# Rearranging the first batch's hand-over, the filters' return and the last tile of a Fourier-mixing and GELU kernel

## The chip, the cores and the metric

The kernel runs on one core of a Trainium2 chip. The metric is device microseconds of one execution. Before the change three runs took 752.50, 753.77 and 754.98 us; their median is 753.77. One more execution was profiled: it took 753.29 us, of which the profile's span covers 751.5.

The core has engines that run side by side, each with its own queue of instructions in order: TensorE (PE, with weight loads shown as PEld), VectorE (DVE), ScalarE (ACT), GpSimd (POOL) and SyncE (SP), which here only issues DMA transfers. POOL issues DMA transfers too: those that change the type on the way (the inputs are fp32, the kernel's tiles bf16 or fp16). All transfers run on the same 16 DMA engines. Matrix products are written to PSUM, which has eight banks; from there DVE or ACT bring them to SBUF ("evacuate" them).

## The reference

Eight batches of 3008 tokens with 256 channels. A real Fourier transform over the tokens is multiplied by a complex filter per frequency and channel, and transformed back. The result goes through two matrix products with an exact GELU between them:

```
X = rfft(x, axis=1);  y = irfft(X * (filt_r + i filt_i), n=3008, axis=1)      # (8, 3008, 256)
h = y.reshape(24064, 256) @ w_in                                              # w_in (256, 2048)
out = (0.5 * h * (1 + erf(h / sqrt(2)))) @ w_out                              # w_out (2048, 256)
```

## The kernel before

**The transform as four stages of matrix products.** 3008 is 47 x 64. A batch goes through a product with a 47-point table (stage 1), a product with the 64-point table and the twiddles (stage 2), the filter, and the two stages back (3 and 4). Between stages 1 and 2, and between 3 and 4, the data are turned round: for batches 1 to 7 by writing them to DRAM (`R1`, `R2`) and reading them back in another order.

- `s1(b, c)`, stage 1, part c of 4: eight matmuls into four PSUM banks, of which one has the tag "h" and three "f"; four evacuations into the tile `a_sb` (L385, pool `pa`, three buffers); four stores to `R1` on SP's queue (L402).
- `r1(b, c)` reads `b_sb` back from `R1` (L408, SP).
- `s2(b, p)`, p from 0 to 11: two matmuls (L416), then on DVE one product of their result with the filters `F` (L419), into a tile `p12` (pool `pp`, six buffers). Product p needs filters 2p and 2p+1 of 24.
- `s3`, `s3_out`: stage 3 and its stores to `R2` (L445); `r2` reads `d_sb` back (L452); `s4` is stage 4 (L461), which ends in `y_sb`, a ring for two batches.

**Batch 0** has functions of its own (`c1`, `c1t`, `c2`, `c3`, `c3t`, `c4`) that turn the data round on PE by transposes, and builds the tables at the same time. `c2(p)` is its product with the filters (L505), on DVE. Its table of stage 3, `T3`, is made in three parts of eight: `table_3` (transposes on PE), `table_3_copy` (to SBUF), and `table_3_turn`, which makes `T3i` out of `T3` by two multiplications by +1 or -1 (L287, on DVE). `warm_up` issues matmuls on a tile of ones, whose result nobody uses.

**The filters.** `load_filters` brings 24 complex filters per channel into rows 0 to 63 of `F` (POOL's DMA queue, L95). For batch 0 `dup_filters` copies them to rows 64 to 127, two filters at a time (L118). Batches 1 to 7 need them in another order of rows: `save_filters` stores rows 0 to 63 to DRAM (`Fd`, L106, SP), and `load_filters_again(k0, k)` reads filters k0 to k0+k-1 back in the new order, in eight transfers (L113, SP). These overwrite `F`, so they wait until batch 0's `c2` is done with the filters in question.

**The two products.** The tokens are cut into 47 tiles of 512. `mm1(t, jc)` makes one sixteenth of h for tile t: two matmuls of 512 columns (L575) into a bank of tag "h" (three banks), and the GELU on ACT (L578). The second product of a tile, `mm2` (L602), takes 64 matmuls of 256 columns. For tiles 1 to 45 it is `mm2_seven` (L662) in its place: a block product by seven multiplications in place of eight (112 matmuls of 128 columns), which needs sums and differences of quarters of the activations, made on DVE (`sums_1`, L632; `sums_2`, L638; `sums_3`, L645) and of the weights (`weight_sums`, L618, once). Its products are added up on DVE out of two PSUM banks of tag "o" (L675 to L685), and stored. The last tile, 46, has `mm2` with a special end: its last quarter is computed in two halves of 128 columns, each stored by itself (L590 to L596, `store`).

**The order.** Nothing is scheduled by a tool. After batch 0's own stages, the main loop (L872) runs over slots, 16 per tile. Slot 16t + jc first calls what the table `at` has for it, then one sixteenth of tile t-1's second product, then `mm1(t, jc)`. `put(slot, f, ...)` fills the table; within a slot the calls run in the order of the `put`s. Those of batch 1 come first (L834): `s1` at slots 0, 4, 8 and 12, `r1` at 15 for parts 0 to 2, `s2` from slot 22 on (product 4 at slot 34), `r2` at 59, `s4` from 67 on, every 0.75 slots. Then come the last tables, the second part of the filters' return and the weight sums at slot 17. The program's order is the order on each engine's queue.

Of the kernel before, what the change touches and what calls it, by code (L numbers as in the profile page):

```python
# [10 lines left out]
ALU = mybir.AluOpType  # L11
FP32 = mybir.dt.float32
# [10 lines left out]
TCH = 512  # L23
# [7 lines left out]
class _Mix:  # L31
# [251 lines left out]
    def table_3_turn(self, q):  # L283

        k = slice(8 * q, 8 * q + 8)
        for r in range(2):
            self.nc.vector.tensor_scalar(out=self.T3i[:, k, r, :], in0=self.T3[:, k, 1 - r, :],  # L287
                                         scalar1=self.turn[r], scalar2=None, op0=ALU.mult)
# [91 lines left out]
    def s1(self, b, c):  # L380

        nc = self.nc
        if c == 0:
            self.st[b, "R1"] = self.dram.tile([NB, 48, 256], BF16, tag="R1", name="R1")
        a = self.pa.tile([128, 2, 4, 256], BF16, tag="a", name="a_sb")  # L385
        x = self.st[b, "x"]
        ps = [[self.bank("ps_s1", "h" if i == h == 0 else "f") for h in range(2)] for i in range(2)]
        for i in range(2):
            for r in range(2):
                for h in range(2):  # L390
                    w = 8 * c + 4 * r + 2 * i
                    nc.tensor.matmul(ps[i][h][64 * r:64 * r + 64, :], lhsT=self.T1s[64 * h:64 * h + NA],  # L392
                                     rhs=x[64 * h:64 * h + NA, w:w + 2, :], start=True, stop=True)
        for i in range(2):
            for h in range(2):
                self._evac(a[:, h, 2 * i:2 * i + 2, :].rearrange("p a b -> p (a b)"), ps[i][h],
                           "act" if h and (b > 1 or i) else False)
        o = self.st[b, "R1"].rearrange("n q c -> q n c")
        for r in range(2):
            for h in range(2):  # L400
                w = HB * h + 8 * c + 4 * r
                nc.sync.dma_start(out=o[:, w:w + 4, :], in_=a[64 * r:64 * r + 48, h])  # L402
# [177 lines left out]
    def mm2(self, t, s):  # L580
# [3 lines left out]
        last = t == self.B * self.S // TCH - 1  # L584
        if last and tile_i == 3:

            half = q // 2
            if q % 2 == 0:
                self.st["o"] = self.bank("ps_e", "o")
            ps = self.st["o"][:, 0:128]  # L590
            for jc in range(8 * (q % 2), 8 * (q % 2) + 8):
                nc.tensor.matmul(ps, lhsT=g[:, jc, 384:512], rhs=self.w_out_sb[:, jc, 128 * half:128 * half + 128],
                                 start=(jc == 0), stop=(jc == 15))
            if q % 2 == 1:
                self.store(t, 3, ps, slice(128 * half, 128 * half + 128))
            return  # L596
# [7 lines left out]
        if last and s == 11:  # L604
            self.store(t, 2, ps[:, 0, :], slice(0, 256))
        elif s % 8 == 7:
            ost = self.po.tile([128, 2, 256], FP32, tag="ost", name="ost")
            nc.vector.tensor_copy(out=ost, in_=ps)
            r0 = t * TCH + (tile_i - 1) * 128
            nc.sync.dma_start(out=self.out[r0:r0 + 256, :].rearrange("(s p) o -> p s o", p=128), in_=ost)  # L610
# [36 lines left out]
    def mm2_seven(self, t, s):  # L647
# [7 lines left out]
               (s31[:, :, 1], q[:, 0]), (a22, q[:, 3]), (s4, w[:, 1, 1]))  # L655
        for n in range(7 * s, 7 * s + 7):
            m, sub, i = n // 16, n // 8 % 2, n % 8
            if n % 16 == 0 and (m == 0 or m % 2 == 1):
                self.st["o"] = self.bank("ps_o", "o").rearrange("p (m s o) -> p m s o", m=2, s=2)
# [4 lines left out]
            if n % 16 != 15 or m % 2:  # L664
                continue
# [10 lines left out]
            elif m == 2:  # L676
                v(out=c(0, 0), in0=t1, in1=p0, op=ALU.add)  # L677
                v(out=t1, in0=t1, in1=p1, op=ALU.add)
            elif m == 4:
                v(out=t3, in0=t1, in1=p0, op=ALU.subtract)  # L680
                v(out=c(1, 1), in0=t3, in1=p1, op=ALU.add)
                v(out=t1, in0=t1, in1=p1, op=ALU.add)
# [7 lines left out]
    def store(self, t, tile_i, ps, cols):  # L690
        ost = self.po.tile([128, 2, 256], FP32, tag="ost", name="ost")
        o = ost[:, 0, 0:cols.stop - cols.start]
        self.nc.vector.tensor_copy(out=o, in_=ps)
        r0 = t * TCH + tile_i * 128
        self.nc.sync.dma_start(out=self.out[r0:r0 + 128, cols], in_=o)
# [3 lines left out]
def kernel(  # L699
# [50 lines left out]
    m.dup_filters(nc.gpsimd, 4, 20)  # L750
    for k in (12, 0):
        m.save_filters(k, 12)
# [3 lines left out]
    for u in range(16):  # L756
# [12 lines left out]
        if u == 11:  # L769
            m.table_2_swap(1)  # L770
            m.table_4(m.T4c, m.T1q, m.wtc, "n", False)
            m.table_3_turn(0)
            m.warm_up(1)
    m.table_3(1)
    m.dup_filters(nc.scalar, 0, 2)
    m.table_3_copy(1, False)
    m.dup_filters(nc.vector, 2, 2)
    m.warm_up(1)
    m.c1t(0, (False, False))
    m.c1t(1, (act,))  # L780
    m.c2(0)
    m.table_3_turn(1)
# [4 lines left out]
    for q in range(1, 7):  # L787
# [7 lines left out]
        if q < 6:  # L795
            m.c3(2 * q - 2)
            if q == 2:
                m.load_filters_again(0, 8)
# [35 lines left out]
    for b in range(1, B):  # L834
        hi = first(b)
        if b == 1:
            s1, n1, r1, s2, n2, group, r2, s4, n4 = 0, 4, 15, 22, 2.5, 12, 59, 67, 0.75
# [24 lines left out]
    put(11, m.table_4_all, g)  # L862
    put(17, m.load_filters_again, 8, 16)
    put(17, m.weight_sums)
    seven = range(1, NT - 1)
# [45 lines left out]
```

## Time and profile before

| what | value |
|---|---|
| median of three runs | 753.77 us |
| profiled execution | 753.29 us |
| its span in the profile | 751.5 us |
| PE busy | 740.1 us, 98% of the span |
| DVE busy | 585.8 us, 78% |
| ACT busy | 545.8 us, 73% |
| POOL busy | 100.8 us, 13%, some two thirds of it in the first 72 us |
| mean granted clock of PE | 0.995 |

The profile names groups of instructions by the line of the kernel, the engine and the tiles: "PE ps_h L575" is the matmul of line 575 that writes the PSUM tile `ps_h`. A releaser, after an arrow, is the instruction or transfer whose end let a waiting one start. "SPq" is the issue of a transfer on SP's queue; "DMA R<-a_sb" is the time until such a transfer has landed. Matmuls overlap: one of 128 columns is listed with 219 ns, but seven in a row take 0.39 us, so the pitch, not the listed duration, is what counts for PE.

In time order: batch 0 and the tables fill the first 38.8 us. There PE, DVE and ACT wait for each other in turn, and `warm_up` keeps PE active. From 38.8 us on the slots run. Batch 1's stages lie among the first 80 slots, up to some 120 us. The DMA engines are nearly full for the first 80 us (x, the filters, both weights, the filters' trip to DRAM and back, batch 1's `R1`). After that each batch runs the same way until the last tile's second product, which begins at 741.7 us and has no first product beside it.

### The profile page before, as it was taken

The numbers are of one execution on the slowest core, as the hardware profiler recorded it, in microseconds if no ns is written. First come the engines' busy times: TensorE is split into PE (matmuls) and PEld (weight loads), VectorE is DVE, ScalarE is ACT, GpSimd is POOL, SyncE is SP. The second block draws the span as 40 slices with busy tenths as digits, with TensorE's granted clock in tenths as the row PEclk, the third lists the DMA queues.
The fourth block names the chain that finished last, engine by engine and source line by source line (L and its number), as shares of the span: only waits on it lengthen the run. The fifth ranks groups of instructions, "written<-read, shape, count | busy, mean of one in ns | idle before, by whom it ended". The sixth has DMA issues, their size and how long they took to land.

```text
span 751.5 us, 20173 instructions
## 1 busy us (share of the span) xinstructions
PE 740.1 (98%) x8388; PEld 518.9 (69%) x8388; DVE 585.8 (78%) x1051; ACT 545.8 (73%) x963; POOL 100.8 (13%) x191
## 2 busy tenths in 40 slices
PE   8989999999999999999999999999999999999998
PEld 4836666766777667667777677666677766777776
DVE  7958977898788977789777997779967798666562
ACT  7866678767786677866777667876678767777773
POOL 7987000021000200012000120002100000000000
PEclk9989999999999999999999999999999999999999
DMA  9999563374434653546526456255562432501011
GB/s 148 225 214 243 149 141 91 115 167 106 113 102 144 151 123 76 142 140 136 123 82 174 106 111 165 58 152 120 122 146 72 135 104 74 127 29 58 30 57 57
DMA packets 91804, 90.71 MB, mean 121 GB/s; under 512 B 7744, under 2 KB 78528, under 8 KB 91456
## 3 DMA queue, kind: packets, MB, share of 16 engines
q1 hardware_dynamic: 83328, 73.43, 35.6%
q0 software_dynamic: 8384, 16.00, 14.0%
q8 instruction: 65, 1.06, 0.6%
q14 instruction: 27, 0.22, 0.1%
HBM read 57.15 MB, written 48.23 MB: 140 GB/s over the span
## 4 chain that ended last, share of the span: by engine, by line
PE 84%; DMA 8%; DVE 4%; POOL 1%; issue 1%; ACT 1%; SPq 1%; DVEq 0%; POOLq 0%; ACTq 0%
PE ps_h L575 38%; PE ps_o L662 34%; PE ps_s L433 3%; PE ps_s L461 3%; PE ps_s L416 2%; DMA R<-a_sb 2%; PE ps_o L602 2%; PE ps_s L392 2%; DVE p L419 2%; DMA F<-Fd 1%; DVE s_sb L632 1%; DMA Fd<-F 1%; DMA w_in_sb<-in_moe_w_in_dram 1%; DMA d_sb<-R 1%; DMA x_sb<-in_x_dram 1%; DMA R<-v_sb 1%
## 5 line engine op out<-in xcount | busy, mean ns | idle before, releaser
L578 ACT ACTIVATE g_sb<-ps_h 128x512 f16<-128x512 f32 x752 | 448.4, 598 | 184.4 <-PE ps_h L575 181.7
L575 PE MATMUL ps_h<-y_sb,w_in_sb 128*128 128x512 bf16 (+3 forms) x1600 | 447.9, 367 | 2.9 <-DVE a_sb L302 2.9
L662 PEld LDWEIGHTS <-g_sb 128*128 128x128 f16 x2880 | 190.2, 98 | 78.7 <-issue 15.6
L662 PEld LDWEIGHTS <-s_sb 128*128 128x128 f16 x2160 | 147.5, 98 | 51.3 <-issue 2.9
L575 PEld LDWEIGHTS <-w_in_sb 128*128 128x128 bf16 x1600 | 124.9, 98 | 10.2 <-issue 5.2
L662 PE MATMUL ps_o<-w_sums,g_sb 128*128 128x128 f16 x1440 | 124.7, 219 | 0.0
L662 PE MATMUL ps_o<-w_sums,s_sb 128*128 128x128 f16 x1440 | 124.5, 219 | 0.0
L632 DVE TENSOR_TENSOR s_sb<-g_sb 128x1024 f16<-128x1024 f16 x180 | 119.4, 686 | 0.0
L662 PE MATMUL ps_o<-w_out_sb,g_sb 128*128 128x128 f16 x1440 | 118.4, 219 | 0.3
L419 DVE TENSOR_TENSOR p<-ps_s,F 128x1024 bf16<-128x1024 f32 x84 | 102.4, 1220 | 17.9 <-PE ps_s L416 16.9
L123 POOL COPY gate<-p 1x1 bf16<-1x1 bf16 x40 | 19.1, 478 | 425.0 <-DVE p L419 425.0
L638 DVE TENSOR_TENSOR g_sb<-s_sb,g_sb 128x1024 f16<-128x1024 f16 x90 | 61.7, 685 | 1.1
L662 PE MATMUL ps_o<-w_out_sb,s_sb 128*128 128x128 f16 x720 | 62.2, 219 | 0.0
L645 DVE TENSOR_TENSOR s_sb<-g_sb 128x1024 f16<-128x1024 f16 x90 | 61.3, 681 | 0.0
L302 DVE CAST a_sb<-ps_s 128x512 bf16<-128x512 f32 x60 | 38.5, 685 | 18.6 <-PE ps_s L392 13.9
L304 DVE TENSOR_SCALAR y_sb<-ps_s 128x376 bf16<-128x376 f32 x56 | 30.5, 545 | 28.8 <-PE ps_s L461 28.8
L461 PEld LDWEIGHTS <-d_sb 96*128 96x128 bf16 x448 | 31.5, 98 | 26.9 <-issue 1.9
L680 DVE TENSOR_TENSOR t_sb<-t_sb,ps_o 128x256 f32<-128x256 f32 x45 | 18.7, 417 | 40.0 <-PE ps_o L662 40.0
L677 DVE TENSOR_TENSOR ost<-t_sb,ps_o 128x256 f32<-128x256 f32 x45 | 18.8, 418 | 31.3 <-PE ps_o L662 31.3
L685 DVE TENSOR_TENSOR ost<-t_sb,ps_o 128x256 f32<-128x256 f32 x90 | 33.6, 414 | 7.4 <-PE ps_o L662 7.4
L461 PE MATMUL ps_s<-T4a,d_sb 96*128 96x94 bf16 x448 | 37.4, 206 | 0.9 <-DMA d_sb<-R 0.9
L86 POOL DMA_DIRECT2D x_sb<-in_x_dram x64 | 33.0, 520 | 2.5 <-issue 2.5
(149 smaller groups left out, 515.1 us busy)
## 6 DMA issues: line engine op xcount, KB each, us to landing
out_dram<-ost SPq DMA_DIRECT2D x93, 256.0 KB, 2.8
x_sb<-in_x_dram POOLq DMA_DIRECT2D x64, 188.0 KB, 3.7
R<-a_sb SPq DMA_DIRECT2D x112, 96.0 KB, 2.2
b_sb<-R SPq DMA_DIRECT2D x28, 384.0 KB, 4.2
R<-v_sb SPq DMA_DIRECT2D x84, 128.0 KB, 2.4
d_sb<-R SPq DMA_DIRECT2D x56, 192.0 KB, 3.9
F<-Fd SPq DMA_DIRECT2D x8, 256.0 KB, 8.3
Fd<-F SPq DMA_DIRECT2D x8, 192.0 KB, 7.7
```

Source lines behind the costliest of these rows:

```text
L86: nc.gpsimd.dma_start(out=xt[h * o:h * o + NA, w:w + 8, :], in_=xv[h][:, w:w + 8, :])
L302: self.nc.vector.tensor_copy(out=out, in_=in_)
L304: self.nc.vector.tensor_scalar(out=out, in0=in_, scalar1=scale, scalar2=None, op0=ALU.mult)
L419: nc.vector.tensor_tensor(out=w, in0=ps.unsqueeze(1).to_broadcast([128, 2, 512]), in1=self.F[:, :, 2 * p:2 * p + 2, :].rearrange("p t a b ...
L461: nc.tensor.matmul(ps[:, 94 * i:94 * i + 94], lhsT=d[:, (grp % 2) * 4 + i, 128 * half:128 * half + 128], rhs=self.T4a[:, 4 * grp + i], sta ...
L575: nc.tensor.matmul(ps[:, o:o + n], lhsT=self.w_in_sb[:, dc, jc * 128:jc * 128 + 128], rhs=self.ring[:, dc, off:off + n], start=(dc == 0), ...
L578: nc.scalar.activation(out=self.st["g", t][:, jc, :], in_=ps, func=AF.Gelu)
L632: self.nc.vector.tensor_tensor(out=self.st["s", t][:, i:i + 2], in0=a, in1=b, op=ALU.subtract)
L638: self.nc.vector.tensor_tensor(out=a21[:, k], in0=self.st["s", t][:, k, 0], in1=a22[:, k], op=ALU.add)
L645: self.nc.vector.tensor_tensor(out=self.st["s4", t][:, k], in0=a12[:, k], in1=s2[:, k], op=ALU.subtract)
L662: nc.tensor.matmul(ps[:, (m + 1) % 2, sub, :], lhsT=a[:, i, 128 * sub:128 * sub + 128], rhs=b[:, i], start=i == 0, stop=i == 7)
L685: v(out=c(h, 1 - h), in0=tt, in1=p, op=ALU.add)
```

## The change

1. `s1(1, 3)`, batch 1's last part of stage 1, writes its evacuations into two tiles of the pool `pp` (the product tiles `p12`) instead of an `a_sb` tile.
2. The return of filters 0 to 7, which stood among batch 0's stages, moves into the slots, in two pieces of four filters: slot 13 and slot 15, the latter behind `r1`. Each piece is eight transfers, so that the return takes 24 transfers instead of 16. On SP's queue the order is now: batch 1's 16 stores of stage 1, eight returns, three `b_sb`, eight returns, and the eight returns of filters 8 to 23.
3. `table_3_turn(1)` runs on POOL, right behind batch 0's `table_3_copy(1)`. The copies of filters 4 to 23 (also POOL) come behind it in the queue; those of filters 0 to 3, of which ACT had one and DVE one, are both on DVE. `c1t(0)` is evacuated half by DVE and half by ACT instead of by DVE alone. One `warm_up` stands a little earlier.
4. Batch 1's `s4` starts at slot 68 instead of 67, with 0.68 instead of 0.75 slots between its 16 calls.
5. The last tile takes `mm2_seven` like the others. There products 5 and 6 are computed in halves of eight matmuls, each half in an output bank of its own, added up and stored by itself (`finish`); the finished quarters of the output are stored early (`store`).

```
     def s1(self, b, c):
...
-        a = self.pa.tile([128, 2, 4, 256], BF16, tag="a", name="a_sb")
+        if b == 1 and c == 3:
+            a = [self.pp.tile([128, 2, 512], BF16, tag="p12", name="p12").rearrange("p i (j c) -> p (i j) c", j=2)
+                 for h in range(2)]
+        else:
+            a = self.pa.tile([128, 2, 4, 256], BF16, tag="a", name="a_sb")
+            a = [a[:, 0], a[:, 1]]
...
     nc.gpsimd.memset(m.vt[:, :, 96, :], 0.0)
-    m.dup_filters(nc.gpsimd, 4, 20)
-    for k in (12, 0):
-        m.save_filters(k, 12)
...
-            m.table_3_turn(0)
+            m.table_3_turn(0, nc.vector)
             m.warm_up(1)
     m.table_3(1)
-    m.dup_filters(nc.scalar, 0, 2)
+    m.dup_filters(nc.vector, 0, 4)
+    m.warm_up(1)
+    m.c1t(0, (False, act))
     m.table_3_copy(1, False)
-    m.dup_filters(nc.vector, 2, 2)
-    m.warm_up(1)
-    m.c1t(0, (False, False))
+    m.table_3_turn(1, nc.gpsimd)
+    m.dup_filters(nc.gpsimd, 4, 20)
+    for k in (12, 0):
+        m.save_filters(k, 12)
     m.c1t(1, (act,))
     m.c2(0)
-    m.table_3_turn(1)
...
-            if q == 2:
-                m.load_filters_again(0, 8)
...
-            s1, n1, r1, s2, n2, group, r2, s4, n4 = 0, 4, 15, 22, 2.5, 12, 59, 67, 0.75
+            s1, n1, r1, s2, n2, group, r2, s4, n4 = 0, 4, 15, 22, 2.5, 12, 59, 68, 0.68
...
+    put(13, m.load_filters_again, 0, 4)
+    put(15, m.load_filters_again, 4, 4)
     put(17, m.load_filters_again, 8, 16)
     put(17, m.weight_sums)
-    seven = range(1, NT - 1)
+    seven = range(1, NT)
...
     def mm2_seven(self, t, s):
...
+        last = t == self.B * self.S // TCH - 1
         for n in range(7 * s, 7 * s + 7):
             m, sub, i = n // 16, n // 8 % 2, n % 8
-            if n % 16 == 0 and (m == 0 or m % 2 == 1):
+            if n % 16 == 0 and (m == 0 or m % 2 == 1) or last and m > 4 and i == 0:
                 self.st["o"] = self.bank("ps_o", "o").rearrange("p (m s o) -> p m s o", m=2, s=2)
...
-            if n % 16 != 15 or m % 2:
+            if last and m > 4 and i == 7:
+                self.finish(t, m, sub, ps)
+            if n % 16 != 15 or m % 2 or last and m > 4:
                 continue
...
+    def finish(self, t, m, sub, ps):
+        h = 6 - m
+        c, tt = self.st["c"][h], self.st["t"][:, h]
+        k = slice(128 * (1 - h), 128 * (1 - h) + 128)
+        self.nc.vector.tensor_tensor(out=c[:, sub, k], in0=tt[:, sub], in1=ps[:, (m + 1) % 2, sub], op=ALU.add)
+        r0 = t * TCH + 256 * h + 128 * sub
+        self.nc.sync.dma_start(out=self.out[r0:r0 + 128, k], in_=c[:, sub, k])
```

## The prediction

> **What bounds the kernel now.** I read the page first: TensorE (PE) is busy for 740.1 of 751.5 us, so at most 11 us can be saved by closing gaps. The slices of the page, then stretches of a few microseconds, show where the gaps lie. In the table by stretches the columns are busy time (and count) of PE, of PE's weight loads, VectorE (DVE), ScalarE (ACT) and GpSimd (POOL), the granted clock, the DMA share and GB/s:
>
> ```profile
> 46.00:48.00 2.00, 2.00 (x14) 0.65 (x13) 0.00 (x0) 1.33 (x4) 1.92 (x3) 1.00 1.32 214
> 48.00:50.00 2.00, 0.27 (x2) 0.00 (x0) 0.00 (x0) 0.00 (x0) 1.84 (x3) 1.00 1.31 215
> 50.00:52.00 2.00, 0.85 (x3) 0.30 (x3) 1.60 (x3) 1.57 (x3) 1.92 (x3) 0.52 1.30 230
> ...
> 56.00:58.00 2.00, 2.00 (x12) 1.26 (x11) 2.00 (x2) 0.96 (x2) 1.92 (x3) 0.77 0.14 27
> 58.00:60.00 2.00, 2.00 (x15) 1.17 (x12) 1.49 (x2) 1.43 (x3) 1.92 (x2) 1.00 0.92 307
> ```
>
> PE stands still from 48.27 to 51.15 (2.88 us), and then runs at half clock until about 56.9: 5.75 us at half speed are another 2.9 us. Together 5.8 us. DMA is full until about 55, and all but idle only from 56 to 58. The chain of waits says why PE stood (start us, us, what):
>
> ```profile
> 32.96 9.74 DMA F<-Fd
> 42.70 0.02 issue
> 42.72 7.56 DMA R<-a_sb
> 50.28 0.03 issue
> 50.31 0.05 DVEq L302
> 50.36 0.04 issue
> 50.40 0.70 DVE a_sb L302
> 51.10 0.04 issue
> 51.15 1.01 PE ps_h L575 x2
> ```
>
> The fourth part of batch 1's first stage (slot 12) needs the `a_sb` buffer of the first part. That buffer's stores stand on SP's queue behind the return of filters 0 to 7 (F<-Fd), and SP's waits list them as released by landings of F<-Fd: a transfer there waits for the one eight places ahead. So the gap is a queueing one. The later steps on SP's queue, from its timeline:
>
> ```profile
> 56.77 1.29 SPq L408 DMA_DIRECT2D b_sb<-R  x3
> 58.11 5.20 SPq L113 DMA_DIRECT2D F<-Fd  x8
> ```
>
> The first b_sb landed 3.3 us after its issue, at 60.1, and PE's first product of batch 1 (slot 22, L416) started at 60.26, without a wait. The last eight F<-Fd landed 6.0 to 10.0 us after issue, the last at 71.9; the first product that needs them runs on DVE at 73.30.
>
> **Edit 1: the fourth part into two product tiles, and filters 0 to 7 returned behind it.** The 7.56 us wait on R<-a_sb leaves the path: two of six product tiles, long free, take its place. In the timeline before, PE ran that part's matmuls at 46.34, so three DVE casts of 0.61 us each end at about 48.85 instead of 52.3. PE then reaches slot 16 at 49.0 (gelus of 0.6 us set the pace) and slot 22 six slots of 0.87 us later (four matmuls of 0.109 and two of 0.216), at 54.2.
>
> What is late next is b_sb. SP now holds, in this order: four stores, eight F<-Fd of filters 0 to 3, three b_sb, eight F<-Fd of filters 4 to 7, eight of filters 8 to 23: 24 returns instead of 16, and eight of them ahead of b_sb. From 48.9: four stores at 0.43 (the pitch of 52.31 to 53.66 before) end at 50.6; eight issues at 0.45 would end at 54.2, and the last four must first see the last stores land (3.0 to 3.5 us after issue), which is about as late. So b_sb is issued near 54.3 and lands 3.3 us later, at 57.6. PE, there at 54.2, waits 3.4 us: the old wait has moved eight slots on. If DMA has less to carry at that time the landing could be 1.5 us earlier; if the small returns (64 KB, for which no row exists) cost as much as the 128 KB ones (1.0 us apart while shared) instead of by bytes (0.3 us, from 8.9 us for eight of 256 KB), it is up to 2.5 us later.
>
> Does that wait cost the clock again? In the stretch from 46.68 to 50.10 PE was busy for 1.59 of 3.42 us, and the clock halved at its end; from 5.72 to 9.14 it was busy for 2.10 and kept the clock. A wait of 3.4 us leaves less than 1.6 us of work in some such stretch unless its phase is lucky. So I count the clock as lost for 5.1 us (between 3.4 and 6.8): 2.6 us. At slot 34: 57.6, plus 12.45 us (60.26 to 72.71 before), plus 2.6, is 72.65 against 72.71. Edit 1 alone gives about 0. With the clock kept it gives 2.6, and with a short wait up to 4.5.
>
> The Trainium skill (TensorE: Matmul & The Clock Gate, Part 1) speaks of at least one idle window of about 3.4 us before the clock drops. The row of this trace differs: 2.88 us of idleness, and a stretch that was 46% busy, were enough. By the page a wait of under 3.4 us would cost no clock and the sum would be 2.6 us lower.
>
> **Edit 2: turns on GpSimd, copies behind them.** The turns (L287, two DVE operations, 0.25 us apart) leave DVE, and the copies of filters 4 to 23 now follow them on POOL. Two rows matter, DVE's and POOL's:
>
> ```profile
> 17.86 3.59 DVE L505 TENSOR_TENSOR p<-ps_c,F 128x1024 bf16<-128x1024 f32 x3
> 18.03 3.98 POOL L118 COPY F<-F 64x1024 bf16<-64x1024 bf16 x4 [1.04 <-DMA F<-in_filt_i_dram]
> ```
>
> DVE's third product of batch 0 starts at 19.09, just as the first copy ends (19.06). The 0.5 us freed on DVE, and the half of `c1t` moved to ACT in exchange for its copy, therefore buy nothing: the copy could not start before its filters landed at 17.9. What can be lost is there: ACT's copy of the table ends near 16.85, POOL's clearing of vt at 16.98, then two turns of 128x512. Their price on POOL is not in the trace. Rows on both sides:
>
> ```profile
> L319 POOL COPY T2p<-T 128x768 bf16<-128x768 bf16 x4 | 3.1, 825 | 0.0
> L376 POOL TENSOR_TENSOR t_sb<-t_sb 96x376 f32<-96x376 f32 x16 | 14.0, 894 | 2.0 <-ACT t_sb L300 1.4
> L333 POOL TENSOR_SCALAR pick<-cols,p 128x128 bf16<-128x128 f32 x1 | 0.6, 632 | 0.1
> ```
>
> By the copy's rate a turn of 512 elements is 0.56 us, by the two-input row (0.19 fixed, as for one element, and 0.70 for 375 more) 1.15, by the 128x128 comparison (0.44 for 127 more) 1.95. I take 0.8, between the first two, which are nearest in size: one bf16 input like the copy, with arithmetic on top. The turns then end at 18.6, the first copy at 19.6, and the chain of DVE products, which runs without a gap to 30.5, is 0.55 us late (0.1 to 2.85). All of batch 0 behind it shifts by that: PE's first gelu matmul from 38.84 to 39.4, and slot 12 with it. The x loads behind the copies on POOL shift too, by less, since the copies also wait for filters at 22.5; DMA has room there (share 0.75 to 0.89 from 28 to 32).
>
> The Trainium skill (GPSIMD Engine Reference, 4.1 Engine selection) keeps elementwise work on VectorE, which speaks against this edit; one-input operations it calls roughly line-rate. The best loop that its section 3.1 states, 1.8 cycles an element, would make an estimate of 0.77 us a turn, and a sum within 0.1 us of mine; no run here shows one yet.
>
> **Edit 3: batch 1's last stage a slot later** (67 to 68, spacing 0.68). The chain shows PE waiting for its input there:
>
> ```profile
> 100.42 4.01 DMA d_sb<-R
> 104.43 0.14 issue
> 104.56 0.51 PE ps_s L461 x8
> ```
>
> PE's gap is 0.77 us; one slot more of work (0.82) covers it. Gain 0.77 (0 if a later d_sb, which lands up to 107.65, is met instead).
>
> **Edit 4: seven products in the last tile.** PE's work falls from 7.04 us (48 matmuls in 5.24, 32 in 1.80) to 112 x 0.056 = 6.25. But at 741.70 DVE still has 0.35 us of the tile before, then five sums (0.60 each, rows L632, L638, L645) and six evacuations (0.375): 5.6 us, near 6.0 with its waits on PE. There are two output banks: product 5's second half needs the one that the third evacuation of product 4 frees, so PE, there after 5.2 us, waits until 6.05; 24 matmuls (1.34), and the last evacuation (0.29, row L693) end at 7.75. Before it was 7.35. So the end is 0.4 us later (0.8 earlier if DVE were never in the way, 0.9 later with sums of 0.69). The last store is 64 KB both times and lands 1.5 us on.
>
> **Sum.** 0.55 (edit 2) - 0.05 (edit 1) - 0.77 + 0.4 = +0.1 on the profiled 753.29 (span 751.5 and 1.8 around it): 753.4. The three runs have 753.77 as median, 0.5 above; half of that kept, 753.6. The likeliest is thus no change that can be told.
>
> **Rivals.** (A) The forecast: a second wait takes the place of the first. By itself 751.8 to 755.8. (B) The second wait is short or keeps the clock: b_sb 1 to 1.5 us earlier, or a lucky phase. For it: DMA was idle from 56 to 58, so its total leaves 2 us; against: eight returns stand ahead of b_sb. It gives -2.6 to -3.5: near 750.6. (C) The return becomes the bound: 16 transfers, not eight, follow b_sb, and product 4 on DVE (73.30 before) needs the last of 24. By bytes the last lands at 71.9 - 2.5 + 8 x 0.3 = 71.8, in time; at 1.0 us each, with those ahead of b_sb late too, near 77.4. DVE has no gap from 66.6 to 80.8, so what exceeds 73.3 goes through to PE: +4, or 757.6. It decides from about 0.7 us a small return. (D) The turns at 1.95 us each: +2.3, near 755.8; it only adds to the others.
>
> **Chances.** A 0.43, B 0.36, C 0.21, with D spread over them. About 0.3%, 2.3 us, is what a measurement of this kernel can tell from no change: below 751.5 is faster, above 756.0 slower. B lies all but wholly below and A all but wholly between: faster 0.37, same 0.42, slower 0.21. The range takes in most of B and a part of C: 749.6 to 756.6.
>
> **What would show it.** No gap at slot 14 near 48; L118 on POOL starting near 18.6; a PE gap ahead of the first L416-type product (57 to 59), released by b_sb, with a second stretch at clock 0.5; no gap ahead of the last stage's first matmul near 104; at the end a PE wait of about 0.8 us between product 5's halves. I am wrong if PE passes slot 22 without a wait, or if F<-Fd lands past 74.

## The result and the profile after

The changed kernel takes 756.75 us (median of four runs, 756.10 to 756.99), the kernel before in the same job 753.39 (752.50 to 754.98). The ratio is 1.0041, with a 95% interval of 1.0022 to 1.006: slower by 3.1 to 3.4 us, where the prediction had 753.6 and "no change" as the likeliest. The profiled execution took 756.71 us, its span 754.9; before it was 753.29 and 751.5, so the two traces show the same difference, 3.4 us. Of all executions behind the ratios below one, of run i1, took 3317.52 us and is left out.

Read in order of time, the trace after says where that is. First the turns, in the groups of GpSimd (POOL) from 15 to 24 us by shape, and behind them the timelines of POOL and DVE (start, us, engine, line):

```profile
L287 POOL TENSOR_SCALAR T<-T,turn_r 128x512 bf16<-128x512 bf16 x1 | 1.6, 1586 | 0.5 <-ACT T L300 0.5
L287 POOL TENSOR_SCALAR T<-T,turn_i 128x512 bf16<-128x512 bf16 x1 | 1.6, 1558 | 0.0
```

```profile
20.43 3.99 POOL L118 COPY F<-F 64x1024 bf16<-64x1024 bf16 x4
```

```profile
21.50 3.49 DVE L510 TENSOR_TENSOR p<-ps_c,F 128x1024 bf16<-128x1024 f32 x3 [3.09 <-POOL F L118]
```

A turn is 1.57 us on POOL, not 0.8. The first copy starts at 20.43 instead of 18.03, DVE's third product at 21.50 instead of 19.09, 2.41 us late, and so does everything behind it: PE's first gelu matmul comes at 41.25 instead of 38.84, late by 2.41 again.

Then the hand-over. The table by stretches of the trace after (columns as before), with SP's timeline of the same time and PE's waits from 36 to 125 us:

```profile
46.00:48.00 2.00, 1.98 (x14) 0.68 (x13) 1.65 (x3) 1.96 (x6) 1.44 (x2) 1.00 1.27 248
48.00:50.00 2.00, 2.00 (x14) 0.67 (x14) 1.02 (x3) 1.97 (x6) 1.84 (x3) 1.00 0.95 267
...
56.00:58.00 2.00, 0.76 (x6) 0.24 (x3) 0.38 (x1) 1.12 (x2) 1.92 (x3) 1.00 0.50 145
58.00:60.00 2.00, 0.00 (x0) 0.00 (x0) 0.00 (x0) 0.00 (x0) 1.92 (x3) 0.74 0.96 277
60.00:62.00 2.00, 1.60 (x7) 1.02 (x8) 0.98 (x1) 0.00 (x0) 1.84 (x3) 0.50 1.02 394
62.00:64.00 2.00, 1.78 (x7) 1.03 (x7) 0.66 (x2) 0.60 (x1) 1.92 (x3) 0.50 0.87 214
64.00:66.00 2.00, 2.00 (x9) 1.13 (x8) 1.41 (x2) 0.60 (x1) 1.92 (x3) 0.56 1.00 250
```

```profile
53.16 3.70 SPq L113 DMA_DIRECT2D F<-Fd  x8
56.96 1.32 SPq L413 DMA_DIRECT2D b_sb<-R  x3
58.37 8.08 SPq L113 DMA_DIRECT2D F<-Fd  x16
```

```profile
PE ps_s L421 <- DMA b_sb<-R: 3.6, 1, 3.6
```

The stop at 48 us is gone, as predicted. A stop of 3.64 us (56.76 to 60.40) for `b_sb` has taken its place, and the clock is lost behind it, from 58.95 to 65.78. That is the likeliest case of the prediction, and yet it is worse than before in one respect. Before, the stop and the lost clock lay *ahead* of `b_sb`, which landed at 60.12; PE arrived at 60.26. There the half clock was all but free. In the experiments below the kernel before was executed 129 times: 37 executions had a mean granted clock of 1.000 and took 752.89 us on average, 17 had 0.995 (some 7 us at half clock) and took 753.37, only 0.5 more. Now `b_sb` lands at 60.26 and the slow clock lies *behind* it: product 4's matmuls start at 75.32 instead of 72.55. The last return lands at 74.31 instead of 71.91.

Stage 4's gap of 0.77 us is gone. When batch 2's first stage begins, the kernel is 2.14 us late, 0.27 less than at the first gelu; at the last gelu 2.18. So from the first gelu to batch 2 the new hand-over costs 0.50 (the 0.77 saved at stage 4, less the 0.27). The rest is at the end. The chain of waits after, last part:

```profile
746.22 2.64 PE ps_o L653 x44
748.86 0.02 issue
748.88 0.43 DVE t_sb L675
749.32 0.02 issue
749.34 0.42 DVE ost L676
749.76 0.34 DVE t_sb L679
750.10 0.05 issue
750.15 1.62 PE ps_o L653 x24
```

From the last gelu to the last evacuation it is 8.17 us instead of 7.32 (+0.85), because the 24 matmuls of the end wait for DVE's third evacuation of product 4 to free a bank. The end of the span comes 1.28 us behind the last landing instead of 0.91 (+0.37, found in every kernel that has the new end, and in none that hasn't; no trace shows why). With the landing itself the time behind the last evacuation is 0.40 longer. Sum: 2.41 - 0.27 + 0.04 + 0.85 + 0.40 = 3.4.

### The profile page after: what moved, and what is told of

The parts are those of the page before. It is cut to its first block, busy times and chain, and to the rows that moved or that the text cites. A ratio compares the mean times of both kernels' runs of the same rounds, so it can differ in the third digit from the quotient of the medians.

```text
span 754.9 us, 20124 instructions
## 1 busy us (share of the span) xinstructions
PE 730.8 (97%) x8284; PEld 518.7 (69%) x8420; DVE 592.9 (79%) x1063; ACT 545.5 (72%) x963; POOL 104.4 (14%) x193
## 4 chain that ended last, share of the span: by engine, by line
PE 87%; DVE 5%; DMA 2%; issue 2%; ACT 2%; POOL 1%; SPq 1%; DVEq 0%; POOLq 0%
PE ps_o L653 37%; PE ps_h L580 36%; PE ps_s L466 3%; PE ps_s L438 3%; PE ps_s L421 3%; PE ps_s L397 2%; DVE p L424 2%; ACT g_sb L583 1%; DVE s_sb L622 1%; PE ps_o L594 1%; DMA x_sb<-in_x_dram 1%; PE ps_c L528 1%; DVE ost L682 1%; DMA d_sb<-R 1%; DMA R<-v_sb 1%
## 5 line engine op out<-in xcount | busy, mean ns | idle before, releaser
L580 PE MATMUL ps_h<-y_sb,w_in_sb 128*128 128x512 bf16 (+3 forms) x1468 | 418.6, 366 | 0.3
L653 PEld LDWEIGHTS <-g_sb 128*128 128x128 f16 x2944 | 193.9, 98 | 81.0 <-issue 15.6
L653 PEld LDWEIGHTS <-s_sb 128*128 128x128 f16 x2208 | 150.3, 98 | 51.4 <-issue 2.9
L653 PE MATMUL ps_o<-w_sums,g_sb 128*128 128x128 f16 x1472 | 127.3, 219 | 2.1 <-DVE t_sb L679 0.9
L653 PE MATMUL ps_o<-w_sums,s_sb 128*128 128x128 f16 x1472 | 126.5, 219 | 1.2
L653 PE MATMUL ps_o<-w_out_sb,g_sb 128*128 128x128 f16 x1472 | 120.4, 219 | 1.8
L622 DVE TENSOR_TENSOR s_sb<-g_sb 128x1024 f16<-128x1024 f16 x184 | 122.0, 687 | 0.0
L628 DVE TENSOR_TENSOR g_sb<-s_sb,g_sb 128x1024 f16<-128x1024 f16 x92 | 63.3, 688 | 1.1
L635 DVE TENSOR_TENSOR s_sb<-g_sb 128x1024 f16<-128x1024 f16 x92 | 62.8, 683 | 0.0
L302 DVE CAST a_sb<-ps_s 128x512 bf16<-128x512 f32 x57 | 36.6, 686 | 14.0 <-PE ps_s L397 13.9
L421 PE MATMUL ps_s<-b_sb,T2p 128*128 128x256 bf16 x168 | 32.5, 276 | 4.7 <-DMA b_sb<-R 3.6
```

The lines of the kernel that those rows point to most:

```text
L302: self.nc.vector.tensor_copy(out=out, in_=in_)
L421: nc.tensor.matmul(ps[:, 256 * i:256 * i + 256], lhsT=self.T2p[:, k].rearrange("p a b c d -> p (a b c d)"), rhs=self.st[b, "b", k // 6][:, ...
L580: nc.tensor.matmul(ps[:, o:o + n], lhsT=self.w_in_sb[:, dc, jc * 128:jc * 128 + 128], rhs=self.ring[:, dc, off:off + n], start=(dc == 0), ...
L622: self.nc.vector.tensor_tensor(out=self.st["s", t][:, i:i + 2], in0=a, in1=b, op=ALU.subtract)
L628: self.nc.vector.tensor_tensor(out=a21[:, k], in0=self.st["s", t][:, k, 0], in1=a22[:, k], op=ALU.add)
L635: self.nc.vector.tensor_tensor(out=self.st["s4", t][:, k], in0=a12[:, k], in1=s2[:, k], op=ALU.subtract)
```

## The experiments

Eighteen kernels were run, each in five rounds beside the kernel before on the same chip. "Ratio" is to that kernel (interval in brackets); 0.1% is 0.75 us. The kernel before took between 752.82 and 753.44 us in these jobs, so times in us of different jobs are compared through the ratios. A profile is one execution, and not always a typical one: that of e1 was the slowest of twelve (757.52), that of h2 the slowest of eleven (754.58), that of b4 the fastest of twelve (752.71).

| run | kernel | median us | before | ratio |
|---|---|---|---|---|
| e1 | change, turns and copies as before | 755.26 | 753.44 | 1.0026 [1.0017, 1.0036] |
| e2 | change, last tile as before | 756.79 | 753.44 | 1.0045 [1.0031, 1.0058] |
| e3 | change, batch 1's products 4 slots later | 756.48 | 753.44 | 1.0039 [1.0026, 1.0053] |
| e4 | change, one of two turns on DVE | 755.65 | 753.44 | 1.0036 [1.0024, 1.0048] |
| b1 | before + hand-over and return (edit 1) | 754.29 | 752.82 | 1.0020 [1.0011, 1.0029] |
| b2 | before + stage 4 later (edit 3) | 751.98 | 752.82 | 0.9993 [0.9984, 1.0002] |
| b3 | before + new last tile (edit 4) | 753.85 | 752.82 | 1.0015 [1.0006, 1.0023] |
| b4 | before + turns on POOL (edit 2) | 753.73 | 752.82 | 1.0015 [1.0006, 1.0025] |
| g1 | e3, batch 2's x loads put later | 755.80 | 753.11 | 1.0033 [1.0021, 1.0045] |
| g2 | b1 + b2, batch 2's x loads put later | 753.68 | 753.11 | 1.0008 [0.9997, 1.002] |
| g3 | before + product tiles alone | 752.74 | 753.11 | 0.9997 [0.9988, 1.0005] |
| g4 | b1, return of 0 to 7 in one piece | 755.05 | 753.11 | 1.0027 [1.0016, 1.0039] |
| h1 | b1 + 13 idle matmuls at slot 21 | 754.64 | 752.83 | 1.0023 [1.0014, 1.0032] |
| h2 | b1, x loads held back | 752.62 | 752.83 | 0.9996 [0.9987, 1.0005] |
| h3 | b1 + b2 + h1 + h2 | 753.32 | 752.83 | 1.0010 [1.0000, 1.0021] |
| h4 | product tiles + b2 | 752.63 | 752.83 | 0.9995 [0.9985, 1.0004] |
| i1 | change, x loads held back | 756.65 | 753.14 | 1.0051 [1.0038, 1.0064] |
| i2 | product tiles + b2, x loads held back | 752.22 | 753.14 | 0.9990 [0.9980, 1.0000] |

### Undoing parts of the change (e1 to e4)

On the changed kernel. In e1 the copies also go back to their old places and engines, in e2 `mm2`, `mm2_seven` and `store` are those of before, in e4 the turn takes the one part `r` that it is to do.

```
e1
-    m.table_3_turn(1, nc.gpsimd)
...
     m.c2(0)
+    m.table_3_turn(1, nc.vector)
e2
-    seven = range(1, NT)
+    seven = range(1, NT - 1)
e3
-            s1, n1, r1, s2, n2, group, r2, s4, n4 = 0, 4, 15, 22, 2.5, 12, 59, 68, 0.68
+            s1, n1, r1, s2, n2, group, r2, s4, n4 = 0, 4, 15, 26, 2.5, 11, 60, 68, 0.68
e4
-    m.table_3_turn(1, nc.gpsimd)
+    m.table_3_turn(1, nc.gpsimd, (0,))
...
     m.c2(0)
+    m.table_3_turn(1, nc.vector, (1,))
```

> The changed kernel with the whole of edit 2 undone: both turns on VectorE after the first product, copies of filters 4 to 23 first on GpSimd, first copies and the first transposes' evacuation as before. Theory 1 (the turns cost 1.58 us each on GpSimd and delay the chain of products from 19.1 to 21.5): third product at 19.1 again, first gelu matmul near 38.8, first b_sb 2 to 2.4 us earlier, time lower by 2.0 to 2.6 us than the changed kernel's 756.7, that is 754.1 to 754.7. Theory 2 (the filters' return is the bound, the last return lands where it does because of 24 transfers): the last return lands within 1 us of 74.3 and the time falls by less than 1 us.

> The changed kernel with edit 4 undone: the last tile has the four-quarter form of before. Theory 1 (in the last tile VectorE's queue and two output banks cost more than the 0.8 us that PE saves): the time from the last gelu to the last evacuation goes from 8.17 back to 7.3 us, and the time falls by 0.8 to 1.3 us, to 755.4 to 755.9. Theory 2 (the tail is a wash): less than 0.4 us.

> The changed kernel with batch 1's filter products four slots later (first at slot 26 instead of 22, groups 11 instead of 12 slots apart, d_sb reads at slot 60 instead of 59). Theory 1 (PE's wait of 3.6 us at slot 22 for b_sb, with the half clock after it, is a wait for a latency chain on SP's queue, and work can be put into it): no PE gap near 57 to 60, no second stretch at half clock, and a time lower by 3.4 to 6.4 us, 750.3 to 753.3; the lower end only if product 4 does not meet the last return (74.3). Theory 2 (transfers bound everything to 75 us): product 4 on VectorE not before 74.3, and less than 1.5 us gained.

> The changed kernel with one of the two turns back on VectorE (after the first product), one on GpSimd ahead of the copies. Theory 1: the third product starts 1.58 us earlier than in the changed kernel, at 19.9, and the time falls by about 1.6 us (1.2 to 2.0). Theory 2: the position of the turns on GpSimd's queue does not set the end; under 0.7 us.

Measured: without the turns on POOL the change is 1.1 us (by the ratios) to 1.5 us (by the medians) better, with one of them moved back 0.4 to 1.1. That is less than the 2.4 us that the turns delay, and the intervals overlap that of the whole change, so no single gain here is clear of noise. The traces show what takes over. DVE's product 4 is the first that needs the last returned filters. In the changed kernel it starts at 75.75, with no idle time before it; in e1:

```profile
74.51 1.22 DVE L424 TENSOR_TENSOR p<-ps_s,F 128x1024 bf16<-128x1024 f32 x1 [1.40 <-PE ps_s L421]
```

PE, the releaser that is named, had been done since 72.27; the last return landed at 74.23 (74.31 in the changed kernel, so this sign is theory 2's). In e1, e2, e3, g1, g2, h1 and h3 DVE stands idle ahead of product 4 and starts it 0.27 or 0.28 us behind the last landing of the return; with the return in its old place no kernel waits there. In the whole change the return is not yet the limit, but it is only 1.2 us away (74.31 plus 0.27, against 75.75): time won ahead of product 4 is kept up to there, unless the return comes earlier too.

e2 gave nothing by the medians, although its trace has the old end of 7.32 us again; the intervals are wide enough to hold the 1.2 us. Its profiled execution began later (first gelu matmul at 42.41) and had its last return at 76.03, which is taken up below. e3 removed the wait for `b_sb`, kept the clock in its profiled execution (its four others were granted 0.997), and gained 0.3: theory 2's number. Product 4 waited 1.68 us for the last return, and the chain of e3 says what held it next:

```profile
75.32 11.28 DMA R<-v_sb
...
102.45 3.82 DMA d_sb<-R
```

The first stores to `R2` (L450) took up to 11 us to land. Transfers, not PE, had become the limit there.

### Each edit alone (b1 to b4)

On the kernel before, one part of the change's diff at a time.

```
b1   (with the new s1)
-                m.load_filters_again(0, 8)
...
+    put(13, m.load_filters_again, 0, 4)
+    put(15, m.load_filters_again, 4, 4)
b2
-            s1, n1, r1, s2, n2, group, r2, s4, n4 = 0, 4, 15, 22, 2.5, 12, 59, 67, 0.75
+            s1, n1, r1, s2, n2, group, r2, s4, n4 = 0, 4, 15, 22, 2.5, 12, 59, 68, 0.68
b3   (with the new mm2, mm2_seven, store, finish)
-    seven = range(1, NT - 1)
+    seven = range(1, NT)
b4   (with the copies behind it, as in the change)
-    m.table_3_turn(1)
+    m.table_3_turn(1, nc.gpsimd)
```

> The kernel before with only the hand-over changed (fourth part of stage 1 into two product tiles, filters 0 to 7 returned in two pieces of eight transfers at slots 13 and 15). Theory 1 (the losses read one by one from the trace of the changed kernel add up; the wait only moves from slot 14 to slot 22 and the clock is lost once either way): 753.4 to 754.1, a gap ahead of the first matmul of batch 1's stage 2 of 2 to 4 us released by b_sb. Theory 2 (eight more return transfers and the later last return are the main cost; DVE's product 4 waits for the last F<-Fd, and the stores to R2 and the read of batch 2's x behind it are late too): 755 to 756, last F<-Fd after 73, DVE's product 4 after 74.

> The kernel before with only batch 1's stage 4 moved (slot 68, spacing 0.68). Theory 1: the gap of 0.77 us ahead of the first L461 matmul goes, 752.5 to 753.0. Theory 2 (a later d_sb, landing up to 107.65, is met instead, or the time is taken elsewhere): 753.2 to 754.

> The kernel before with only the last tile's second product by seven products. Theory 1: from the last gelu to the last evacuation 8.2 us in place of 7.3, and the end of the span 0.4 us further behind it: 754.2 to 754.7. Theory 2 (run e2, which took this edit back without any gain in time, shows what it costs): 753.2 to 753.7.

> The kernel before with only the second pair of turns on GpSimd and the copies of filters 4 to 23 behind it. Theory 1 (two turns of 1.57 us delay the copies by 2.4 us, the chain of DVE products and all behind it shift by as much): first gelu matmul at 41.2 and 755.4 to 755.9. Theory 2 (the delay in batch 0 is hidden later, because PE stands at slot 14 until stores behind the filters' return have landed, and transfers until 72 us set when product 4 runs): first gelu matmul at 41.2 too, the gap ahead of slot 14 shorter than 2.9 us, and 753.4 to 754.4.

Alone they cost +1.5, -0.5, +1.1 and +1.1 us by the ratios, each give or take 0.7, +3.2 together, against 3.1 for the whole. The hand-over, predicted at nothing, is the largest by the ratios, though the intervals overlap. The kernel before was 0.57 us faster in this job than in the first; allowing for that, b2 and b3 are theory 1's, b4 is theory 2's, and b1 lies between its two, near theory 2 by its time, but with its last return at 72.61, not after 73. b3's trace has the same +0.85 and +0.37 as the whole change. b4's first gelu matmul is at 41.23, as late as after, and at batch 2's first stage nothing is left of the delay (119.85 against 119.83). PE's waits in b4 from 36 to 125 us:

```profile
PE ps_s L416 <- DMA b_sb<-R: 1.8, 1, 1.8
PE ps_h L575 <- DVE a_sb L302: 1.2, 1, 1.2
```

The old stop at slot 14 is 1.2 us instead of 2.9, and the clock was kept. So in this execution the delay was hidden in a stop that ended at its own time; where the 1.1 us of the other executions lie, no trace shows. Why the delay can't hide in the whole change is seen by putting all 20 profiled kernels into two groups (us):

| return of filters 0 to 7 | first gelu matmul | first `b_sb` issued | last F<-Fd landed |
|---|---|---|---|
| among batch 0's stages (7 kernels) | 38.2 to 41.2 | 55.8 to 57.6 | 70.8 to 72.7 |
| of these b4, turns on POOL | 41.23 | 56.56 | 71.48 |
| moved into the slots (13 kernels) | 38.8 to 43.3 | 15.5 to 16.5 behind it | 72.1 to 77.0 |
| of these b1 | 39.14 | 54.86 | 72.61 |
| of these after | 41.25 | 56.96 | 74.31 |

With the old order `b_sb` comes when the transfers are through, whenever batch 1 starts. With the new order the return and `b_sb` follow batch 1's stores, and every delay of the start goes through to both (the last return lands 32.9 to 35.1 us behind the first gelu matmul in all 13). Edit 1 brings `b_sb` 1.9 us forward (b1), and edit 2 takes 2.1 back.

### Which half of the hand-over costs (g1 to g4)

g1 is e3, g2 is b1 with b2, each with the x loads put later (g2 from slot 44 on); g3 is the change's `s1` alone; g4 is b1 with its return in one piece.

```
g1
-                put(unit(i + 2) if b > 1 else 25, m.load_next, b, i + 2, i // 2, i % 2)
+                put(unit(i + 2) if b > 1 else 48 + int(2.5 * i), m.load_next, b, i + 2, i // 2, i % 2)
g4
-    put(13, m.load_filters_again, 0, 4)
-    put(15, m.load_filters_again, 4, 4)
+    put(13, m.load_filters_again, 0, 8)
```

> Run e3 (the changed kernel with batch 1's products four slots later, 756.48) with batch 2's eight loads of x moved from slot 25 to slots 48 to 65. Theory 1 (two limits lie close together: b_sb with the lost clock, and the transfers, which are full until 82 to 86 us because the x loads of batch 2 run beside the filters' return and the first stores to R2; e3 took the first away and met the second, 11.28 us of DMA R<-v_sb in its chain): those stores take 2 to 4 us, the gaps after 80 us go, 752.9 to 755.0. Theory 2 (the middle of the kernel is not bound by transfers, e3 gained nothing for another reason): 756 to 757.

> The kernel before with the hand-over of the change and its later stage 4, and batch 2's x loads at slots 44 to 61; turns and last tile as before. Theory 1: b1 (754.29) without its 1.48 us wait of DVE's v_sb for R<-v_sb and without the gap ahead of stage 4, 751.5 to 753.0, so it beats the kernel before by 0 to 1.5 us. Theory 2: as b1 and b2 together, 753.5 to 754.2.

> The kernel before with the fourth part of stage 1 in two product tiles and nothing else; the return of filters 0 to 7 stays among batch 0's stages, as eight transfers. Theory 1 (the loss of the hand-over lies in the return, whose eight more transfers stand ahead of b_sb and go out at SP's pitch of 0.46 us each, with the last landing at 72.6 in b1 although b_sb was issued 1.9 us earlier): b_sb is issued at 53.5 to 55, the gap ahead of stage 2 is under 3 us, the last F<-Fd lands before 71, and the time is 751.0 to 752.8. Theory 2 (the loss lies in the tiles, or in the clock that any wait near 55 costs): 753.5 to 754.5, as b1.

> Run b1 with filters 0 to 7 returned in one piece at slot 13 (eight transfers of 128 KB instead of sixteen of 64 KB). Theory 1 (the number of transfers counts): the last F<-Fd lands 2 to 4 us earlier than in b1 (72.6), b_sb up to 1 us later, 752.8 to 754.0. Theory 2 (bytes count): landings as in b1, 754.0 to 754.8.

g1 and g2 did not test what they were made for. GpSimd issues a load as soon as its queue is empty, and in g2 the x loads went out at 68.5 to 72.2 us, as in the kernel before (67.5 to 71.1), whatever their slot. g3 answers: the product tiles alone cost nothing, so the 1.5 us lie in moving the return. They also win nothing that can be told (two of theory 1's signs failed: `b_sb` was issued at 56.96 and the last return landed at 72.27), and its waits of PE show the next thing behind the old one:

```profile
PE ps_o L607 <- DMA w_out_sb<-in_moe_w_out_dram: 3.2, 2, 2.8
PE ps_s L421 <- DMA b_sb<-R: 1.9, 1, 1.9
```

With the return in its old place the weights of the second product land at 55.04 (48.32 in b1), and PE stands 2.8 us for them where it stood 2.9 for `a_sb`. g4 refutes theory 1 there: eight transfers in place of sixteen were no better. The last return came 0.5 us earlier, `b_sb` 1.7 us later, and PE stood for 5.3 us.

### Clock or transfers (h1 to h4)

`keep_busy` issues matmuls of 128x512 from `w_in_sb` into a PSUM bank that nobody reads. In h2 `load_next` puts a small POOL copy of a product tile ahead of a load, as it does for the later batches, so that POOL's queue waits for that product.

```
h1
+    put(21, m.keep_busy, 13)
h2
     def load_next(self, b, p, c, h):
-        if b > 1:
+        if b > 0:
             self.gate(self.st[b, "p", p][0:1, 0, 0:1])
...
-                put(unit(i + 2) if b > 1 else 25, m.load_next, b, i + 2, i // 2, i % 2)
+                put(unit(i + 2) if b > 1 else unit(i + 4), m.load_next, b, i + 2 if b > 1 else i + 4, i // 2, i % 2)
```

> Run b1 (hand-over and return moved, 754.29) with 13 matmuls whose result nobody uses put on PE's queue at slot 21, 2.8 us at full clock, inside the wait of 3.8 us for b_sb. Theory 1 (the loss of b1 is the clock that this wait costs, 1.7 us in its profiled execution and up to 3.4 in others): no stretch at half clock, 752.0 to 753.0. Theory 2 (the loss lies after it, in the transfers): the clock is kept and DVE's wait for R<-v_sb grows instead, 753.8 to 754.6.

> Run b1 with batch 2's eight x loads held back on GpSimd until products 4 to 11 exist (runs g1 and g2 moved them in the table only, and they were issued as early as before). Theory 1 (clock at the wait for b_sb): 753.9 to 754.5, as b1. Theory 2 (transfers): the first stores to R2 land in 2 to 4 us instead of 11.6, DVE's wait for them of 1.5 us goes, and the time is 752.4 to 753.4.

> b1 with the matmuls of h1, the held loads of h2 and stage 4 at slot 68 as in b2. If the clock and the transfers take turns as the limit (each alone gives little), this one gains what neither gives alone: 749.5 to 751.5, faster than the kernel before. If not, it is b1 and b2 together with what h1 and h2 gain: 752 to 753.5.

> The kernel before with the product tiles (g3, 0.9997) and the later stage 4 (b2, 0.9993) and nothing else of the change. If the parts add up: 0.999, some 752.3. If the gap ahead of stage 4 (0.38 us in g3) was all that was left to win: 752.4 to 753.

The two causes could be told apart. h1 kept the clock at the wait for `b_sb`; from 60 to 62 us the table by stretches has b1 and then h1:

```profile
60.00:62.00 2.00, 2.00 (x8) 0.99 (x7) 0.67 (x2) 0.60 (x1) 1.92 (x3) 0.54 0.71 168
```

```profile
60.00:62.00 2.00, 2.00 (x17) 1.40 (x16) 1.92 (x3) 1.24 (x3) 1.84 (x4) 1.00 0.67 168
```

Eight matmuls at half clock became 17 at full, and PE reached product 4 at 70.91 instead of 72.38. There it lost it again. DVE in h1:

```profile
71.26 0.68 DVE L643 TENSOR_TENSOR s_sb<-g_sb 128x1024 f16<-128x1024 f16 x1
74.09 1.23 DVE L430 TENSOR_TENSOR p<-ps_s,F 128x1024 bf16<-128x1024 f32 x1 [2.15 <-PE ps_h L586]
```

The releaser that is named, PE, had been done for a long time; the last return landed at 73.81. PE then stood 1.93 us for DVE (74.03 to 75.97), the clock was lost behind that stop instead (half from 76.82 to 80.23), and the time did not fall (754.64): theory 2's time, with another wait than the one it named. That trace alone would leave the clock as a cause, but eight of h1's eleven executions had a mean granted clock of 1.000, and they took 754.66 us on average, where b1's eleven took 754.17. h2 did nothing for the clock (lost for 6.8 us in its profiled execution, for 3.4 in b1's) and held batch 2's x loads back. DVE's `v_sb` before the second pair of stores to `R2`, in b1 and then in h2:

```profile
83.71 0.69 DVE L302 CAST v_sb<-ps_s 128x512 bf16<-128x512 f32 x1 [1.48 <-DMA R<-v_sb]
```

```profile
83.40 0.69 DVE L302 CAST v_sb<-ps_s 128x512 bf16<-128x512 f32 x1
```

and the issues from 70 to 86 us (KB each, median us from issue to landing), b1 and h2:

```profile
R<-v_sb SPq DMA_DIRECT2D x6, 128.0 KB, 11.3
```

```profile
R<-v_sb SPq DMA_DIRECT2D x7, 128.0 KB, 2.8
```

h2 is 1.7 us better than b1 by the medians (0.9996 against 1.0020): the whole cost of the hand-over, back by taking 1.5 MB of x out of its way. (Held back with the return in its old place, i2 against h4 below, the same loads give 0.4.) So standing alone, edit 1 pays its price in transfers, not in clock. h3 gained nothing on top: with the clock kept, DVE waits for the last return again (PE stood 2.0 us at 73.5). It lies where its expectation has it if the two limits do not take turns. h4 is no better than its two parts.

### The whole change, and the best version (i1, i2)

Edits of h2, on the changed kernel (i1) and on h4 (i2).

> The changed kernel whole (756.75, 1.0041) with batch 2's x loads held back as in h2. Theory 2 of h1 and h2 (what the moved return costs is collected where the transfers are full, from 72 us on, and h2 got 1.5 us back): the first stores to R2 take 2 to 5 us in place of 10 to 11, and the time is 754.6 to 755.7, ratio 1.0018 to 1.003. Rival (in the whole change the turns have already delayed PE to where the transfers no longer hold it, its trace shows no gap between 61 and 107 us): 756.2 to 757.

> The kernel before with the product tiles, the later stage 4 (h4, 0.9995) and the held x loads; the return, the turns and the last tile as before. If the transfers after 72 us hold this one too (DVE waits 0.9 us for R<-v_sb in h4): 751.3 to 752.3, ratio 0.998 to 0.999, so the best of all. If not: as h4, 752.4 to 753.

i1 gained nothing: the rival is right. The stores to `R2` did land in 4 to 5 us, but in the whole change PE does not wait for them (no gap between 61 and 107 us); it is late by the turns and the clock already. i2 has the lowest ratio of all, 752.22 against 753.14; its interval just reaches no change, and it can't be told from b2, g3, h2 and h4. It keeps the product tiles and stage 4's slot from the change, adds the held loads, and leaves the other edits out.

## Why the prediction was wrong

**Edit 2 is the step that failed by most.** The prediction gave three rows for a turn's price and took 0.8 us, "between the first two, which are nearest in size". That is below both of its rows with arithmetic: two inputs gave 1.15, and the same operation (TENSOR_SCALAR on POOL), scaled from 128x128, gave 1.95. 1.57 was measured, half-way between these two. The delay was 2.41 us in place of 0.55; two turns at 1.57 in place of 0.8 are 1.54 of the difference, and the rest is mostly a later start (17.23 in place of 16.98, behind ACT's copy of the table). Rival (D) was nearest: its 2.3 more make a delay of 2.85. Alone the edit costs 1.1 (b4); the prediction let the delay pass through in full, and in b4's trace it does not. Of the total error of 3.3 us (753.4 to 756.71), 1.86 is this term at the first gelu, 0.55 the hand-over in the whole change (+0.50 for -0.05), and 0.85 the end. The Trainium skill (GPSIMD Engine Reference, 3.1) has a best case of 1.8 cycles an element, which the prediction turned into 0.77 us. This trace has 1.57, twice that.

**Edit 1: right up to slot 34, and not followed further.** "So b_sb is issued near 54.3 and lands 3.3 us later, at 57.6" and "PE, there at 54.2, waits 3.4 us": b1 has 54.86, 58.31 and a wait of 3.79 from 54.65. "At slot 34: 57.6 [...] is 72.65 against 72.71": b1 has 72.38 against 72.55 there. From this it concluded "Edit 1 alone gives about 0", and b1 cost 1.5 us. What failed is the end of the sum at slot 34. Moving a megabyte of return from a time when PE is not waiting for transfers to one when they are full pushes what comes behind it: in b1 batch 2's x loads are through at 84.46 instead of 82.29, and the fourth store to `R2` has landed at 85.04 instead of 83.02. (b1's profiled execution was one of its faster ones, 753.37, so its trace shows the place and not the full price.) That these transfers are the price is what h2 shows. Rival (C), "the return becomes the bound", had the right place, and the wrong test: it was to decide "from about 0.7 us a small return". In b1 the small ones landed 0.2 to 0.5 us apart, and the return still became a limit as soon as PE was earlier (e1, e3, h1, h3). The x loads of batch 2, which share that time and set its end, were not in the working.

**Edit 3** was predicted at -0.77: the gap went, and alone it gives -0.5, with an interval that holds both -0.77 and 0.

**Edit 4** was mis-sized. Predicted +0.4: the PE wait between the halves came as foreseen (0.85 for 0.8), but an earlier one of 0.33 for DVE's `sums_2`, and 0.37 behind the last landing, were not counted. Together +1.25 by the trace, +1.1 alone.

**By its own signs:** no stop at slot 14, a stop at 57 to 60 released by `b_sb`, a second stretch at half clock, no gap ahead of stage 4, a wait of 0.8 in the last tile: all five came. "L118 on POOL starting near 18.6" did not (20.43), and that sign pointed at the term that failed. "F<-Fd lands past 74", by which the prediction called itself wrong, came too (74.31), but as a consequence: DVE's product 4 did not wait for it (PE's matmuls for it ended at 75.70). That the likeliest case (A) came is no proof of the sum: the stop was as long as foreseen (3.64 for 3.4), and everything stood 2.4 us later.

**What stays open.** The four prices add up to the whole, but each is known to 0.7 us only, so this may be chance. Undoing parts gave less (e1 -1.1 to -1.5, e2 and i1 nothing). For e1 and e3 the traces show the limit that takes over, the last return at product 4. For e2 two things are seen. Its profiled execution began later, and its last return came at 76.03, 33.6 us behind the first gelu matmul as in the others. And three of its six executions had a mean granted clock of 0.993 (757.14 us on average), three 0.995 (756.01), where the changed kernel had 0.995 to 0.997; its trace has a second lost stretch of 3.4 us, from 23.42 on. With three executions each this is a hint. What the lost clock behind slot 22 costs the whole change is not known: no run keeps it there and leaves the rest alone.

## What to carry to other kernels

When the price of a moved operation is not in the trace and a chain hangs on it, do not take less than the rows with the same kind of work give: here those were 1.15 and 1.95 us, 0.8 was taken, 1.57 came. Before a wait is removed, ask what else lands at its end: here `a_sb`, the second product's weights, `b_sb`, the last return and the stores to `R2` stood within a few us of each other, and taking one away gave the next. A stop that ends at a fixed time hides what is late ahead of it; an edit that ties its end to the start of the work gives that cover away.

## What was not expected of the hardware

**A turn on DVE has two durations.** In e1's profiled execution the same two operations that took 0.34 and 0.35 us before took 1.15 and 1.12, on DVE. DVE and POOL in e1:

```profile
17.35 1.15 DVE L287 TENSOR_SCALAR T<-T,turn_r 128x512 bf16<-128x512 bf16 x1
18.42 1.12 DVE L287 TENSOR_SCALAR T<-T,turn_i 128x512 bf16<-128x512 bf16 x1
```

```profile
17.32 4.10 POOL L118 COPY F<-F 64x1024 bf16<-64x1024 bf16 x4
```

Before, POOL's first copy began at 18.03, just when the turns were over (17.34 to 17.94). Of 13 profiled kernels with both turns on DVE, four (e1, g2, h4, i2) had turns that began while a copy ran on POOL: those turns took 0.77 to 1.15 us, all others of this pair 0.34 or 0.35, and PE's first gelu matmul came at 40.0 to 40.7 instead of 38.2 to 39.7. The Trainium skill (GPSIMD Engine Reference, 1. Specifications) says that the SBUF interfaces are shared with VectorE, with contention when a DVE instruction runs in a 2-port mode or has two inputs in SBUF. Which mode these turns ran in no run here shows. What the traces show is a wait: each of the seven slow turns ends 0.15 us behind the end of the copy during which it began (e1's first at 18.50, the copy at 18.35), as if it could not work before that. A turn that had begun before the copy kept its 0.34 us (g2's first). In e1's profiled execution DVE's third product came at 20.59 for this reason, instead of 19.09; how often that happens in the other executions is not known.

**The clock depends on more than the length of the wait.** A stop of 3.64 us was followed by 6.8 us at half clock (after), one of 3.79 by 3.4 (b1), and one of 3.76 by none (e1). Nor does the length put them in order: one of 2.17 was followed by 3.4 (h4), one of 3.02 by none (b2). In all 20 traces every lost stretch before the last tile lasts 3.41 or 6.83 us. With the turns on POOL, DVE's wait of 3 us near 20 us also cost the clock in three of six profiled executions (e2, g1, i1: half clock for 3.4 us from 23.4 to 23.8 on, first gelu matmul at 42.4 to 43.3 instead of 41.1 to 41.3). The Trainium skill (TensorE: Matmul & The Clock Gate, Part 1) calls the window free-running, so that the phase decides; these rows agree with it, and no length of a gap alone would have told them apart.
